# A fused attention and feed-forward kernel: its opening and first block reordered

## The chip, the cores and the metric

The kernel runs on 1 core of one Trainium2 chip. The metric is the device time of one execution, in microseconds (us). In the text PE is the matmul engine (TensorE), DVE, ACT and POOL are the vector, scalar and GpSimd engines, and SP is the engine that issues most data transfers (DMAs). POOL issues the weight transfers, which convert fp32 to bf16 on the way.

## The reference, cut to what matters

```python
# q, k, v: (B=8, H=8, S=576, D=64) fp32
def phi(x, c, s):                       # c, s: cos and sin of (pi/2) * pos / S
    r = np.maximum(x, 0.0)
    return np.concatenate([r * c, r * s], axis=-1)          # 64 -> 128 features
q_p = phi(q, cos_w, sin_w);  k_p = phi(k, cos_w, sin_w)
kv  = np.einsum('bhsf,bhsd->bhfd', k_p, v);  z = np.sum(k_p, axis=2)
num = np.einsum('bhsf,bhfd->bhsd', q_p, kv)
den = np.einsum('bhsf,bhf->bhs', q_p, z)[..., None] + 1e-06
x   = (num / den).transpose(0, 2, 1, 3).reshape(B * S, H * D)   # 4608 x 512
xn  = x / sqrt(mean(x * x) + 1e-06) * rms_g
out = (silu(xn @ w_gate) * (xn @ w_val)) @ w_out                # 512 -> 1536 -> 512
```

Each batch has 576 tokens: four chunks of 128 (c = 0 to 3) and a tail of 64 (c = 4).

## The kernel before

The feed-forward part (FFN) works in nine blocks of 512 tokens: one per batch, and a last one of the eight 64-token tails. A block has twelve gate/value steps (n = 0 to 11, eight matmuls of 128x512 each) and then 48 output matmuls. Attention for batch b+1 is computed inside block b, by small jobs that are hung into the steps. Block 0 has no block ahead of it, so an "opening" computes the attention of batch 0 first. Before block 1 can start, block 0 must also have produced the attention of batch 1.

The words used below: `phi` builds q or k features (on DVE and ACT); `kvz` is the key/value product; `nd` is the attention product of one q chunk, followed by `nd_post` (divide), `x_sq` (sum of squares on ACT, power on POOL), `x_norm` (DVE) and `x_tr` (transpose to feed the FFN). The q features must be transposed before `nd`; the result is the tile `qpT`. There are two ways to do it:

```python
def q_tr_dma(b, c):                    # a DMA does it, issued by SP; no engine computes
    nc.sync.dma_start_transpose(out=q_dst(b, c), in_=...)
def q_tr_pe(b, c, bank):               # PE does it, eight 128x128 matmuls into PSUM
    for h in range(H):
        nc.tensor.transpose(dst[:, h, 0:n], t[lo:hi, h, :], ident[lo:hi, lo:hi])
def q_tr_evac(eng, b, c, bank):        # and DVE or ACT copies the result out
    copy(eng, q_dst(b, c), dst[:, :, 0:n])
```

The opening, and the transfers that follow it:

```python
for which in ("k", "q", "v"):          # load batch 0, in this order, on SP
    ...
# ... [cut: k phi, q phi, all q chunks transposed with q_tr_pe]
v_cast(nc.gpsimd, 0, LOW)              # waits for v; the weight issues stand behind it on POOL
gval_slice(0, 256)                     # 12 weight transfers in all, 256 columns each
# ... [cut: kvz, then per 128 tokens: nd, norm, x_tr, open_ffn(j) = steps 0 and 1]

def first_loads_of_1():
    first = load_main("k", k, 1, bufs=two)
    tc.add_manual_dep(first.ins, weight_dmas[9].ins.name, SYNC_DEP, reason="after the weights")
    load_tail("k", k, 1); load("q", 1); load("v", 1)
    ...                                # then w_out in four transfers on POOL, after v
```

The output phase of block 0, in which batch 1's attention is finished:

```python
for n in range(NNT):
    # ... [cut]
    if n == 3:
        kvz_pe(1, psA); ...
    if n in (4, 6, 8, 10):
        nd_pe(1, j, psA); nd_post(1, j, psA); x_sq(1, j); x_norm(1, j)
    if n in (5, 7, 9, 11):             # one output step later, PE needs the result of that chain
        x_tr_pe(1, j, psV[j % 2][:, :]); x_tr_evac(A, 1, j, psV[j % 2][:, :])
    for j in ...: out_mm(0, j, n, banks0[j])
```

From block 1 on, q chunks are transposed by DMA. In the steady blocks the v casts ran on ACT at slot 15, `kvz` at step 6, and the `nd` jobs at steps 7, 9, 11 and 12.

Of the kernel before, what the change touches and what calls it, by code (L numbers as in the profile page):

```python
# [22 lines left out]
def kernel(  # L23
# [11 lines left out]
    nc = tc.nc  # L35
# [42 lines left out]
    def load_tail(which, src, b):  # L78
        lo = 64 * (b % 2)
        t = one.tile([P, H, D], FP32, name=f"r{which}t{b % 2}", tag=f"r{which}t{b % 2}")  # L80
        raw[(which + "t", b)] = t
        return nc.sync.dma_start(
            out=t[lo : lo + 64, :, :],
            in_=src[b, :, 512:576, :].rearrange("h s d -> s h d"),
        )
# [8 lines left out]
    for which in ("k", "q", "v"):  # L94
        bufs = two if which == "k" else one
        load_main(which, src_of[which], 0, (0, 4), bufs)
        load_main(which, src_of[which], 0, (4, 8), bufs)
        load_tail(which, src_of[which], 0)

    gb = one.tile([P, DM], FP32, name="gb")  # L100
    with nc.allow_non_contiguous_dma(reason="rms_g to all partitions"):
        nc.sync.dma_start(
            out=gb[:, :],
            in_=moe_rms_g.rearrange("(o d) -> o d", o=1).to_broadcast([P, DM]),
        )

# [44 lines left out]
    kpt = [one.tile([P, H, F], BF16, name=f"kpt{i}") for i in range(2)]  # L151
# [5 lines left out]
    for i in range(2):  # L157
        other = slice(64, 128) if i == 0 else slice(0, 64)
        mine = slice(0, 64) if i == 0 else slice(64, 128)
        nc.gpsimd.memset(kpt[i][other, :, :], 0.0)  # L160
        nc.gpsimd.memset(vvt[i][other, :, :], 0.0)
        nc.gpsimd.memset(vvt[i][mine, :, D:E], 1.0)
        nc.gpsimd.memset(vvm[i][:, :, :, D:E], 1.0)
# [15 lines left out]

    def half(b):  # L180
        lo = 64 * (b % 2)
        return lo, lo + 64
# [12 lines left out]
    def k_phi(eng, b, c, part, heads=(0, 8)):  # L195

        o = slice(0, D) if part == 0 else slice(D, F)
        f = cos_of if part == 0 else sin_of
        if c < 4:
            if b not in kp_main:  # L200
                kp_main[b] = one.tile([P, 4, H, F], BF16, name="kpm", tag="kpm")
            src = view4(raw[("k", b)], heads)[:, :, c, :]
            phi(eng, kp_main[b][:, c, heads[0] : heads[1], o], src, f(c))
        else:
            lo, hi = half(b)
            phi(eng, kpt[b % 2][lo:hi, :, o], raw[("kt", b)][lo:hi, :, :], f(4, lo, hi))

    def q_phi(eng, b, c, part, heads=(0, 8)):
        o = slice(0, D) if part == 0 else slice(D, F)
        f = cos_of if part == 0 else sin_of  # L210
        if (b, c) not in qp_tiles:
            qp_tiles[(b, c)] = four.tile([P, H, F], BF16, name="qp", tag="qp")
        t = qp_tiles[(b, c)]
        if c < 4:
            src = view4(raw[("q", b)], heads)[:, :, c, :]
            phi(eng, t[:, heads[0] : heads[1], o], src, f(c))
        else:
            lo, hi = half(b)
            phi(eng, t[lo:hi, :, o], raw[("qt", b)][lo:hi, :, :], f(4, lo, hi))

    def q_dst(b, c):
        if b not in qpT:
            qpT[b] = two.tile([P, H, S], BF16, name="qpT", tag="qpT")
        n = P if c < 4 else 64
        return qpT[b][:, :, c * P : c * P + n]

    def q_tr_dma(b, c):
        t = qp_tiles[(b, c)]
        lo, hi = (0, P) if c < 4 else half(b)
        nc.sync.dma_start_transpose(  # L230
            out=q_dst(b, c), in_=t[lo:hi, :, :].rearrange("p h f -> p (h f)")
        )

    def q_tr_pe(b, c, bank):
        t = qp_tiles[(b, c)]
        lo, hi = (0, P) if c < 4 else half(b)
        n = hi - lo
        dst = bank.bitcast(BF16).rearrange("p (h s) -> p h s", h=H)
        for h in range(H):
            nc.tensor.transpose(dst[:, h, 0:n], t[lo:hi, h, :], ident[lo:hi, lo:hi])  # L240

    def q_tr_evac(eng, b, c, bank):
        n = P if c < 4 else 64
        dst = bank.bitcast(BF16).rearrange("p (h s) -> p h s", h=H)
        copy(eng, q_dst(b, c), dst[:, :, 0:n])
# [14 lines left out]
    def v_cast_tail(eng, b):  # L260
        lo, hi = half(b)
        copy(eng, vvt[b % 2][lo:hi, :, 0:D], raw[("vt", b)][lo:hi, :, :])
# [4 lines left out]
    def kvz_pe(b, pst, heads=range(8)):  # L267
        o = headview(pst)
        for h in heads:
            for c in range(5):  # L270
                lhsT = kp_main[b][:, c, h, :] if c < 4 else kpt[b % 2][:, h, :]
# [10 lines left out]
    def nd_pe(b, j, pst):  # L282

        o = headview(pst)
        for h in range(H):
            g, i = h // 4, h % 4
            if j < 4:
                nc.tensor.matmul(  # L288
                    o[:, g, i, :], lhsT=qpT[b][:, h, j * P : (j + 1) * P],
                    rhs=kvzs[b][:, g, i * E : (i + 1) * E], start=True, stop=True,  # L290
                )
            else:
                for bb in (b - 1, b):
                    lo, hi = half(bb)
                    nc.tensor.matmul(
                        o[lo:hi, g, i, :], lhsT=qpT[bb][:, h, 512:576],
# [117 lines left out]
    def filler(n):  # L414
        for _ in range(n):
            nc.tensor.matmul(
                psO[:, 1, :], lhsT=warm[:, 0:P], rhs=warm[:, :], start=True, stop=True
            )


    V, A = nc.vector, nc.scalar
    LOW, HIGH = (0, 4), (4, 8)
    filler(24)
# [6 lines left out]
    qbank = [psG[0][:, :], psG[1][:, :], psV[0][:, :], psV[1][:, :], psO[:, 0, :]]  # L430
    for c in range(4):
        q_phi(V, 0, c, 0, LOW)
        q_phi(A, 0, c, 1, LOW)
    for c in range(4):
        q_phi(V, 0, c, 0, HIGH)
        q_phi(A if c < 2 else V, 0, c, 1, HIGH)
        q_tr_pe(0, c, qbank[c])
        if c >= 1:
            q_tr_evac(V, 0, c - 1, qbank[c - 1])
    v_cast(nc.gpsimd, 0, LOW)  # L440
# [7 lines left out]
    v_cast(V, 0, HIGH)  # L448
    v_cast_tail(A, 0)
    q_tr_evac(V, 0, 3, qbank[3])  # L450
    for i in range(1, 6):
        gval_slice(256 * i, 256 * i + 256)
    kvz_pe(0, psA, range(0, 4))
    kvz_evac(A, 0, psA, 0)
    kvz_pe(0, psA, range(4, 8))
    kvz_evac(A, 0, psA, 1)

    def open_tr(j):
        x_tr_pe(0, j, (psA if j % 2 == 0 else psO)[:, 0, :])
        x_tr_evac(A, 0, j, (psA if j % 2 == 0 else psO)[:, 0, :])  # L460

    def open_ffn(j):
        for n in range(2):
            gval_mm(0, n, n, (j * P, (j + 1) * P))

    nd_pe(0, 0, psA)
    filler(2)
    nd_post(0, 0, psA)
    x_sq(0, 0)
    nd_pe(0, 1, psO)  # L470
    nd_post(0, 1, psO)
    x_sq(0, 1)
    x_norm(0, 0)
    open_tr(0)
    nd_pe(0, 2, psA)
    open_ffn(0)
    nd_post(0, 2, psA)
    x_sq(0, 2)
    x_norm(0, 1)
    open_tr(1)  # L480
    nd_pe(0, 3, psO)
    open_ffn(1)
# [3 lines left out]
    open_tr(2)  # L486
    open_ffn(2)
    x_norm(0, 3)
    open_tr(3)
    open_ffn(3)  # L490
    q_phi(V, 0, 4, 0)
    q_phi(V, 0, 4, 1)
    q_tr_pe(0, 4, qbank[4])
    q_tr_evac(A, 0, 4, qbank[4])
    for n in range(2):
        gval_h(0, n, n, gval_act(0, n, n))
# [22 lines left out]
    def first_loads_of_1():  # L519
        first = load_main("k", k, 1, bufs=two)  # L520
        tc.add_manual_dep(first.ins, weight_dmas[9].ins.name, SYNC_DEP, reason="after the weights")
        load_tail("k", k, 1)
        load("q", 1)
        load("v", 1)
        for i in range(4):
# [5 lines left out]
            if i == 0:  # L531
                tc.add_manual_dep(
                    d.ins, last_load[("v", 1)].ins.name, SYNC_DEP, reason="after batch 1"
                )
# [6 lines left out]
    for c in range(5):  # L541
        at(0, 8 + (c + 1) // 2, "post", q_phi, V, 1, c, 0)
        at(0, 8 + (c + 1) // 2, "post", q_phi, A, 1, c, 1)
        n = (9, 10, 11, 12, 13)[c]
        at(0, n, "pe", q_tr_pe, 1, c, psA[:, c % 2, :])
        at(0, n, "pre", q_tr_evac, V, 1, c, psA[:, c % 2, :])
    at(0, 11, "post", v_cast, A, 1)
    at(0, 11, "post", v_cast_tail, A, 1)


    for nb in range(2, B):
        b = nb - 1
        first = nb == 2
        for c in range(5):
            kb, kn = (b, 1 + (c * 3) // 5) if first else (b - 1, 12 + (c * 3) // 5)
            at(kb, kn, "post", k_phi, V, nb, c, 0)
            at(kb, kn, "post", k_phi, A, nb, c, 1)
            qn = c + 3 if first else c
# [3 lines left out]
        vb, vn = (b, 5) if first else (b - 1, 15)  # L562
        at(vb, vn, "post", v_cast, A, nb, LOW)
        at(vb, vn + 1 if first else vn, "post", v_cast, A, nb, HIGH)
        at(vb, vn, "post", v_cast_tail, A, nb)
        kz = 8 if first else 6
# [3 lines left out]
        for j in range(4):  # L570
            n = ((9, 10, 11, 12) if first else (7, 9, 11, 12))[j]
# [11 lines left out]
    for nb in range(3, B):  # L583
# [3 lines left out]
        at(b, 7 if b == 1 else 2, "pre", load, "v", nb)  # L587
        at(b, 8 if b == 1 else 5, "post", load, "q", nb)

    def gval_step(blk, n):  # L590
        bank = n % 2
# [18 lines left out]
    for n in range(2, NNT):  # L610
        gval_step(0, n)
    banks0 = [psC[0][:, :], psC[1][:, :], psG[0][:, :], psG[1][:, :]]
    for n in range(NNT):
        if n == 0:
            run(0, 12, "pe")
            run(0, 12, "pre")
# [3 lines left out]
        if n == 2:  # L620
            run(0, 13, "pe")
            run(0, 13, "pre")
        if n == 3:
            kvz_pe(1, psA)
            kvz_evac(A, 1, psA, 0)
            kvz_evac(A, 1, psA, 1)
        if n in (4, 6, 8, 10):
            j = n // 2 - 2
            nd_pe(1, j, psA)
            nd_post(1, j, psA)  # L630
            x_sq(1, j)
            x_norm(1, j)
        if n == 5:
            load("v", 2)
            load("q", 2)
        if n in (5, 7, 9, 11):
            j = (n - 1) // 2 - 2
# [6 lines left out]
    run(0, 12, "post")  # L644
    run(0, 13, "post")
    run(0, 14, "post")
    run(0, 15, "post")
# [41 lines left out]
```

## Time and profile before

| | before |
|---|---|
| timed, median of 3 | 373.08 us (373.04 to 374.59) |
| the profiled execution | 369.74 us, of which the profile shows a span of 368.0 us |
| block 1 starts (first gate matmul of it) | 92.53 us |
| blocks 1 to 6 | 34.1, 35.2, 34.3, 35.2, 34.4, 35.2 us |
| blocks 7 and 8 (no attention in them) | 31.1 us each |

Block starts are read from PE's timeline: the first gate matmul after a run of output matmuls. First the head of the page: busy times, then PE's busy share and granted clock in 40 equal slices (9.2 us each), in tenths.

```profile
span 368.0 us, 5659 instructions
...
PE 330.5 (90%) x2122; PEld 163.8 (45%) x2122; DVE 179.4 (49%) x366; ACT 185.8 (50%) x345; POOL 37.7 (10%) x74
...
PE   7628797865999999999999999999999999999995
...
PEclk9655599988999999999999999999999999999999
```

PE is busy nearly everywhere but in the first ten slices. 90% alone would suggest that nothing is to be had; the slices show one poor stretch of 92 us and a dense remainder. What PE waited for in that stretch (engine, line, tile and releaser: us in total, times, longest):

```profile
PE psV L362 <- DVE xn L337: 8.8, 4, 2.7
PE psA L362 <- DVE xn L337: 5.8, 2, 5.6
PE psA L240 <- DVE qp L191: 2.7, 2, 1.3
```

The first line is the output phase of block 0, and the timeline shows one of its four links (start, duration, engine, line, what; in brackets the idle time before it):

```profile
71.21 0.42 PE L288 MATMUL psA<-kvzs,qpT 128*128 128x65 bf16 x8
...
71.73 0.17 DVE L309 TENSOR_SCALAR rec<-psA 128x8 f32<-128x8 f32 x1 [2.99 <-PE psA L288]
...
72.17 0.69 DVE L313 TENSOR_TENSOR xt<-psA,rec 128x512 f32<-128x512 f32 x1
72.96 0.64 ACT L325 ACTIVATE scr<-xt 128x513 bf16<-128x513 f32 x1 [1.80 <-DVE xt L313]
...
73.77 0.56 POOL L330 TENSOR_TENSOR rs<-ms,mhalf 128x1 f32<-128x1 f32 x1 [22.28 <-ACT scr L325]
74.36 0.75 DVE L337 SCALAR_TENSOR_TENSOR xn<-xt,rs,gb 128x512 bf16<-128x512 f32 x1 [1.50 <-POOL rs L330]
...
75.17 0.40 PE L362 MATMUL psV<-ident,xn 128*128 128x128 bf16 x4 [2.68 <-DVE xn L337]
```

From the attention product at 71.21 to the transpose that needs its result at 75.17 are 4.0 us, and PE has only one output step (four matmuls) to fill them with. It stands 2.7 us here, and 8.8 us in the four links together. The phase lasts from 66.06 to 92.53 us for 10.4 us of output matmuls; the waits cost clock as well (0.66 granted from 75 to 80 us).

The clock in that stretch, by windows (the columns are: window, length, busy time of PE, PEld, DVE, ACT, POOL with counts, granted PE clock, DMA share, GB/s):

```profile
10.00:15.00 5.00, 3.25 (x32) 2.61 (x33) 4.51 (x11) 1.13 (x4) 2.59 (x3) 0.63 1.00 266
...
25.00:30.00 5.00, 2.91 (x28) 2.48 (x28) 2.44 (x5) 1.10 (x2) 0.93 (x2) 0.50 1.45 196
...
45.00:50.00 5.00, 5.00 (x23) 2.19 (x22) 2.08 (x3) 1.42 (x3) 1.60 (x3) 0.96 0.14 28
```

The clock is halved from about 11 us (0.63 is the mean over 10 to 15 us) to about 45 us. The Trainium skill, "TensorE: Matmul & The Clock Gate", Part 1, says that the throttled clock is the default and that some 3.4 us of sustained activity release it. This trace agrees: matmuls run without a gap from 41.74 us, and the full clock is back at about 45.4 us.

In the steady blocks, PE's waits from 126.7 to 301 us are two groups, and the q transposes by DMA land in 4.0 us (median from issue to landing):

```profile
PE psA L288 <- DVE xt L313: 3.0, 5, 0.6
PE psG L376 <- ACT sg L385: 1.5, 3, 0.5
```
```profile
qpT<-qp SPq DMA_TRANSPOSE x25, 4.0
```

### The profile page before, as it was taken

To read this page: it belongs to the slowest core of one execution; us is meant where nothing else is said; L and a number is where in the kernel's file an instruction comes from. 1 tells how busy PE (TensorE), PEld (TensorE's weight loads), DVE (VectorE), ACT (ScalarE), POOL (GpSimd) and SP (SyncE) were. 2 spreads that over 40 slices of the span, in tenths; PEclk is the share of its full clock that TensorE was granted. 3 is DMA by queue.
4 is the path that set the end of the run, shared out by engine and by line. 5 is a ranking of instruction groups with operands and counts; after the bars stand their busy time and mean duration, and the time that the engine had idled before them with its cause. 6 is when DMAs were issued, how large, how long until landed. Compare 5 with 4: busy or idle time off the path is not lost.

```text
span 368.0 us, 5659 instructions
## 1 busy us (share of the span) xinstructions
PE 330.5 (90%) x2122; PEld 163.8 (45%) x2122; DVE 179.4 (49%) x366; ACT 185.8 (50%) x345; POOL 37.7 (10%) x74
## 2 busy tenths in 40 slices
PE   7628797865999999999999999999999999999995
PEld 3517443422454445445444544454445444444442
DVE  6635255433859266825772576358255723303320
ACT  5322265422884784576567556853694433313321
POOL 4651030011002000100110011001000110000000
PEclk9655599988999999999999999999999999999999
DMA  8999968630899799559956993999442250011013
GB/s 245 211 189 230 266 93 195 185 89 0 241 138 248 177 219 238 137 149 203 265 110 184 229 206 97 207 210 195 118 106 54 30 157 3 0 57 59 0 28 86
DMA packets 94875, 53.84 MB, mean 146 GB/s; under 512 B 57856, under 2 KB 90112, under 8 KB 94848
## 3 DMA queue, kind: packets, MB, share of 16 engines
q1 hardware_dynamic: 86912, 48.77, 57.3%
q0 software_dynamic: 7936, 4.72, 9.3%
q8 instruction: 16, 0.26, 0.3%
q14 instruction: 11, 0.09, 0.1%
HBM read 38.01 MB, written 9.44 MB: 129 GB/s over the span
## 4 chain that ended last, share of the span: by engine, by line
PE 69%; DVE 10%; ACT 8%; DMA 6%; issue 4%; POOL 2%; SPq 1%; ACTq 0%; DVEq 0%
PE psC L396 24%; PE psG L376 19%; PE psV L376 19%; DVE xn L337 3%; DVE xt L313 3%; PE psA L273 2%; DMA wv<-in_moe_w_val_dram 2%; DMA rv<-in_v_dram 2%; ACT vvm L249 2%; ACT scr L325 2%; PE psA L288 2%; ACT sg L385 1%; DMA rq<-in_q_dram 1%; PE psG L396 1%; DVE rec L312 1%
## 5 line engine op out<-in xcount | busy, mean ns | idle before, releaser
L391 DVE TENSOR_TENSOR hT<-psV,sg 128x512 bf16<-128x512 f32 x108 | 74.5, 690 | 121.4 <-PE psV L376 72.3
L376 PE MATMUL psG<-xnT,wg 128*128 128x512 bf16 (+1 forms) x408 | 102.4, 376 | 4.3 <-ACT sg L385 2.7
L376 PE MATMUL psV<-xnT,wv 128*128 128x512 bf16 (+1 forms) x408 | 102.5, 377 | 0.0
L385 ACT ACTIVATE sg<-psG 128x512 f32<-128x512 f32 x108 | 64.0, 594 | 64.9 <-PE psG L376 64.6
L396 PE MATMUL psC<-wo,hT 128*128 128x512 bf16 x408 | 92.8, 382 | 0.0
L376 PEld LDWEIGHTS <-wv 128*128 128x128 bf16 x456 | 45.4, 102 | 50.7 <-issue 1.1
L376 PEld LDWEIGHTS <-wg 128*128 128x128 bf16 x456 | 43.4, 101 | 49.5 <-issue 7.3
L396 PEld LDWEIGHTS <-hT 128*128 128x128 bf16 x432 | 41.4, 99 | 47.0 <-issue 1.1
L330 POOL TENSOR_TENSOR rs<-ms,mhalf 128x1 f32<-128x1 f32 x36 | 19.9, 555 | 236.4 <-ACT scr L325 236.4
L249 ACT COPY osb<-psC 128x512 f32<-128x512 f32 x33 | 19.3, 586 | 47.5 <-PE psC L396 47.5
L337 DVE SCALAR_TENSOR_TENSOR xn<-xt,rs,gb 128x512 bf16<-128x512 f32 x36 | 26.9, 746 | 21.8 <-POOL rs L330 21.8
L325 ACT ACTIVATE scr<-xt 128x513 bf16<-128x513 f32 x36 | 22.9, 636 | 24.7 <-DVE xt L313 24.5
L313 DVE TENSOR_TENSOR xt<-psA,rec 128x512 f32<-128x512 f32 x34 | 23.5, 691 | 1.2
L189 ACT ACTIVATE qp<-rq,tab 128x512 bf16<-128x512 f32 (+1 forms) x34 | 22.4, 676 | 0.8 <-DMA rq<-in_q_dram 0.7
L189 ACT ACTIVATE kpm<-rk,tab 128x512 bf16<-128x512 f32 (+1 forms) x34 | 21.0, 673 | 1.9 <-DMA rk<-in_k_dram 1.9
L288 PEld LDWEIGHTS <-qpT 128*128 128x128 bf16 x256 | 13.7, 104 | 14.4 <-issue 8.9
L288 PE MATMUL psA<-kvzs,qpT 128*128 128x65 bf16 x240 | 13.5, 201 | 4.7 <-DVE xt L313 3.6
L191 DVE TENSOR_SCALAR qp<-rq,tab 128x512 bf16<-128x512 f32 (+1 forms) x38 | 16.7, 454 | 0.7 <-DMA rq<-in_q_dram 0.7
L191 DVE TENSOR_SCALAR kpm<-rk,tab 128x512 bf16<-128x512 f32 (+1 forms) x38 | 15.2, 448 | 2.4 <-DMA rk<-in_k_dram 2.4
L249 ACT CAST vvm<-rv 128x1024 bf16<-128x1024 f32 (+1 forms) x13 | 14.0, 1113 | 0.1
L309 DVE TENSOR_SCALAR rec<-psA 128x8 f32<-128x8 f32 x34 | 5.5, 161 | 16.6 <-PE psA L288 14.5
L273 PEld LDWEIGHTS <-kpm 128*128 128x128 bf16 x256 | 11.6, 102 | 3.2 <-issue 1.5
(66 smaller groups left out, 177.3 us busy)
## 6 DMA issues: line engine op xcount, KB each, us to landing
out_dram<-osb SPq DMA_DIRECT2D x32, 256.0 KB, 2.4
rk<-in_k_dram SPq DMA_DIRECT2D x7, 1024.0 KB, 6.8
rq<-in_q_dram SPq DMA_DIRECT2D x7, 1024.0 KB, 7.1
rv<-in_v_dram SPq DMA_DIRECT2D x7, 1024.0 KB, 6.7
wg<-in_moe_w_gate_dram POOLq DMA_DIRECT2D x6, 256.0 KB, 8.9
wv<-in_moe_w_val_dram POOLq DMA_DIRECT2D x6, 256.0 KB, 9.6
wo<-in_moe_w_out_dram POOLq DMA_DIRECT2D x4, 384.0 KB, 6.9
rk<-in_k_dram SPq DMA_DIRECT2D x2, 512.0 KB, 4.4
```

Of the source, the lines that this page charges most:

```text
L189: nc.scalar.activation(out=out_ap, in_=in_ap, func=AF.Relu, scale=scale)
L191: nc.vector.tensor_scalar(out=out_ap, in0=in_ap, scalar1=scale, scalar2=0.0, op0=ALU.mult, op1=ALU.max)
L249: nc.scalar.copy(out=o, in_=i)
L288: nc.tensor.matmul(o[:, g, i, :], lhsT=qpT[b][:, h, j * P : (j + 1) * P], rhs=kvzs[b][:, g, i * E : (i + 1) * E], start=True, stop=True,)
L313: nc.vector.tensor_tensor(out=xt[:, 0:DM].rearrange("p (b h d) -> p b h d", b=2, d=D), in0=o[:, :, :, 0:D], in1=rec[:, :, :].unsqueeze(3). ...
L325: nc.scalar.activation(out=scr[:, :], in_=xt[:, 0 : DM + 1], func=AF.Square, scale=1.0 / math.sqrt(DM), accum_out=ms[:, :],)
L330: nc.gpsimd.tensor_tensor(out=rs[:, :], in0=ms[:, :], in1=mhalf[:, :], op=ALU.pow)
L337: nc.vector.scalar_tensor_tensor(out=xn[:, :], in0=x_of[(b, j)][:, 0:DM], scalar=rs_of[(b, j)][:, :], in1=gb[:, :], op0=ALU.mult, op1=ALU. ...
L376: nc.tensor.matmul(pst[bank][:, cols[0] : cols[1]], lhsT=w[:, t, n * P : (n + 1) * P], rhs=x[:, t, cols[0] : cols[1]], start=(t == 0), sto ...
L385: nc.scalar.activation(out=sg[:, :], in_=psG[bank][:, :], func=AF.Silu)
L391: nc.vector.tensor_tensor(out=hTs[blk][:, n, :], in0=psV[bank][:, :], in1=sg[:, :], op=ALU.mult)
L396: nc.tensor.matmul(bank, lhsT=hTs[blk][:, n, j * P : (j + 1) * P], rhs=wo[:, n, :], start=(n == 0), stop=(n == NNT - 1),)
```

## The change

The intent is to start the FFN sooner and to fill the gaps in block 0. It has six parts:

1. Batch 0 is loaded as k, v, q, with q by token pairs. Weights are issued when v has landed; there are 8 transfers (four of 256 columns, then four of 512) for 12.
2. The opening does FFN steps 0 to 3 (before: 0 and 1), with matmuls over 128 or 256 tokens, and ten dummy matmuls (fillers) in two groups stand between its attention products (before: two).
3. q chunks 2 and 3 of batch 0, its tail, and all q chunks of batch 1 are transposed by DMA, no longer by PE.
4. In block 0's output phase, `nd` comes at n = 1, 3, 5, 7 and each `x_tr` four or five output steps later.
5. The 64-token tails are laid out by head halves on 128 partitions.
6. In the steady blocks the v casts go from ACT to DVE and POOL, `kvz` to step 4, `nd` to steps 5, 7, 9, 11.

The diff, cut to its core (the tail layout and the new opening FFN helpers are left out):

```diff
-    for which in ("k", "q", "v"):
+    for which in ("k", "v"):
...
+    load_pair("q", 0, 0)
+    load_pair("q", 0, 1)
...
     gval_slice(0, 256)
+    tc.add_manual_dep(
+        weight_dmas[0].ins, first["v"].ins.name, SYNC_DEP, reason="weights after v"
+    )
+    gval_slice(256, 512)
...
+    for c in (2, 3):
+        q_phi(G, 0, c, 0)
+        q_phi(A, 0, c, 1)
+        q_tr_dma(0, c)
...
-    q_tr_pe(0, 4, qbank[4])
-    q_tr_evac(A, 0, 4, qbank[4])
+    q_tr_dma(0, 4)                       # on SP, ahead of batch 1's loads
...
     def first_loads_of_1():
-        first = load_main("k", k, 1, bufs=two)
-        tc.add_manual_dep(first.ins, weight_dmas[9].ins.name, SYNC_DEP, reason="after the weights")
+        d = load_main("k", k, 1, bufs=two)
+        tc.add_manual_dep(d.ins, weight_dmas[6].ins.name, SYNC_DEP, reason="after the weights")
         load_tail("k", k, 1)
         load("q", 1)
-        load("v", 1)
+        gate = load_main("v", v, 1, LOW)  # w_out is issued when this half has landed
+        load_main("v", v, 1, HIGH)
...
-        n = (9, 10, 11, 12, 13)[c]
-        at(0, n, "pe", q_tr_pe, 1, c, psA[:, c % 2, :])
-        at(0, n, "pre", q_tr_evac, V, 1, c, psA[:, c % 2, :])
+        n = (8, 8, 9, 9, 10)[c]
+        at(0, n, "post", q_tr_dma, 1, c)
...
-        at(vb, vn, "post", v_cast, A, nb, LOW)
-        at(vb, vn + 1 if first else vn, "post", v_cast, A, nb, HIGH)
+        at(vb, vn, "post", v_cast, V, nb, LOW)
+        at(vb, vn + 1, "post", v_cast, V, nb, HIGH)
...
-        if n in (4, 6, 8, 10):
-            j = n // 2 - 2
+        if n in (1, 3, 5, 7):
+            j = n // 2
             nd_pe(1, j, psA)
             nd_post(1, j, psA)
             x_sq(1, j)
-            x_norm(1, j)
...
-        if n in (5, 7, 9, 11):
-            j = (n - 1) // 2 - 2
+        if n in (4, 6, 8, 10):
+            x_norm(1, n // 2 - 2)
+        if n in (6, 8, 10, 11):
+            j = (6, 8, 10, 11).index(n)
             x_tr_pe(1, j, psV[j % 2][:, :])
```

## The prediction

> What bounds it now. The page says PE is busy 90% of 368.0 us. The table of windows and the chain of waits split that in two. In steady blocks PE is the bound: twelve gate/value steps of 1.73 us (8 matmuls) and 10.37 us of output matmuls are 31.1 us, and blocks 7 and 8, which carry no attention, take that. Blocks 2 to 6 take 34.4 or 35.2 us between the ends of their output matmuls, against about 33.7 of matmul work: 0.5 us at each block start waiting for the Silu behind two 1.04 us v casts and a 0.62 us tail cast on ACT, and about 0.6 to 0.9 us at the n=12 attention product waiting for DVE. The opening is the larger loss: block 1 starts at 92.5 us, though block 0 holds some 32 us of matmuls. There: v lands at 12.4 to 14.9 us and only then do weights start; first FFN matmul at 27.9; clock granted 0.50 from 13 to 45 us; q transposes starve PE at 55.8 to 65 (ACT and DVE phi work); the output phase of block 0 takes 66 to 92.5 us for 10.4 us of matmuls, because each link of norm, transpose and attention (about 5 us) is waited for in series.
>
> What the change does. v is loaded second and q last, so weights start at about 10 us instead of 13.4. The q load now overlaps them. Key/value product at about 11, first FFN at about 21 to 22 (estimate: the same DVE, ACT, POOL links, q landing at 12 to 15, two DMA transposes landing about 4 to 6 us after issue). The opening does steps 0 to 3 rather than 0 and 1, in wider 256-column matmuls. Step 4, at 47.2 before, should begin at about 36.
>
> What it costs. On the SP queue the loads of batch 1 now stand behind the tail-q DMA transpose, which waits for the last opening FFN product. So k of batch 1 is issued at about 38 (31.9 before), lands at about 44, q at about 48, v at about 52 (rates as before, 13 us for the three). Its phi work blocks the Silu queue: I expect PE to stall 2 to 5 us around step 8 and again near v. wo, gated on half of v, lands piecewise from about 55 to 60 (48.4 to 59 before).
>
> Output phase of block 0: attention products at n=1,3,5,7, transposes 5 steps later: about 14 us instead of 26. Block 1 then starts at about 69 (64 to 74), 23 us earlier.
>
> Steady: v cast goes to DVE (0.68 a half) and POOL, the attention products all lie in gate/value steps. Both measured stalls should go: about 1.1 us in each of 5 to 6 blocks, 6 us in all.
>
> The Trainium skill ("TensorE: Matmul & The Clock Gate", Part 1) says that the clock is halved by default and released after about 3.4 us of sustained activity. The trace agrees: continuous matmuls from 41.7, full clock by 45.3. A denser opening should regain it near 30.
>
> Sum: 373 - 23 - 6 = 344 us; 80% range 336 to 353. Faster by over 2%: 0.97; within 2%: 0.025; slower: 0.005.
>
> To check: weight issue near 10; step 4 near 36; k of batch 1 issued near 38 with ACT and DVE waiting for it; block 1 start near 69; blocks 2 to 6 near 33.8.
>
> Wrong if: DMA transposes stall the opening under weight traffic; the batch 1 loads come later than I think; PE stays at half clock through the stalls; or DVE becomes the releaser in steady blocks.

## The result, and the profile after

The changed kernel is correct and took 355.43 us (median of 4, 354.07 to 357.78), against 373.83 us for the kernel before in the same rounds. The ratio is 0.9508, with a 95% interval of 0.9443 to 0.9574. A ratio here is the mean time of one kernel's fast runs over that of the other's of the same rounds, so it is not quite the ratio of the medians. The direction was right; the time lies 11.4 us above the 344 predicted and 2.4 us above the range.

| us | before | predicted | after |
|---|---|---|---|
| first weight issue | 13.39 | about 10 | 11.14 |
| first gate/value matmul | 27.95 | 21 to 22 | 23.36 |
| step 4 starts | 46.98 (the prediction read 47.2) | about 36 | 38.11 |
| k of batch 1 issued | 31.89 | about 38 | 41.03 |
| output phase of block 0 | 26.5 | about 14 | 21.0 |
| block 1 starts | 92.53 | 69 | 80.87 |
| blocks 1 to 6 together | 208.5 | 6 less | 205.4 |
| span of the profile | 368.0 | | 353.1 |

The spans differ by 14.9 us, and the table accounts for that: 92.53 - 80.87 = 11.7 us ahead of block 1, and 208.5 - 205.4 = 3.2 us (from the unrounded block times) in the steady blocks. The timed medians differ by more, 18.4 us, because the profiled execution of before was one of its faster ones (369.74 us against a median of 373.83). Block 1 starts 11.9 us after the 69 us predicted, and of the 6 us after it 2.8 us are missing. In sum that is more than the 11.4 us by which the timed median missed, for the same reason: the trace of before is of one of its faster executions.

The head of the page after:

```profile
span 353.1 us, 5619 instructions
...
PE 321.0 (91%) x2052; PEld 159.3 (45%) x2087; DVE 180.0 (51%) x369; ACT 165.4 (47%) x323; POOL 39.0 (11%) x85
...
PE   8557958399899999999899999999999999999994
...
PEclk9976989789999999999999999999999999999999
```

The half-clock stretch of the opening has shrunk from some 34 us to about ten (22 to 32 us), but PE still has holes: the 5s in slices 2, 3 and 6, and the 3 in slice 8. What it waited for ahead of block 1:

```profile
PE psA L302 <- DMA qpT<-qp: 9.7, 3, 5.4
PE psG L391 <- ACT sg L400: 3.9, 1, 3.9
...
PE psO L302 <- DMA qpT<-qp: 1.4, 1, 1.4
```

The waits for DVE's `xn` are gone but for 0.2 us, as intended. In their place are 11.1 us of waits for `qpT` that come from a DMA, which the kernel before did not have ahead of block 1: 3.5 and 1.4 us in the opening, 0.8 and 5.4 us in the output phase. The 3.9 us line is the predicted stall in which ACT, holding batch 1's k features ahead of a Silu, waits for k.

Now the transfers. The issues on SP (start, how long SP was held, what), then those on POOL:

```profile
15.28 5.24 SPq L243 DMA_TRANSPOSE qpT<-qp  x2
39.74 1.19 SPq L243 DMA_TRANSPOSE qtT<-qp  x1
41.03 0.54 SPq L73 DMA_DIRECT2D rk<-in_k_dram  x1
...
53.87 14.88 SPq L243 DMA_TRANSPOSE qpT<-qp  x4
```
```profile
11.14 0.95 POOL L185 DMA_DIRECT2D wg<-in_moe_w_gate_dram  x1 [7.14 <-DMA rvt<-in_v_dram]
...
53.76 3.09 POOL L579 DMA_DIRECT2D wo<-in_moe_w_out_dram  x4 [23.05 <-DMA rv<-in_v_dram]
```

Two things stand in those lines. The tail transpose (`qtT`) is issued at 39.74 and k of batch 1 right behind it, so the end of the opening decides when batch 1 begins to load. And the four q transposes of batch 1 are issued at 53.87, a tenth of a microsecond after the four w_out transfers at 53.76; the issues alone take 14.88 us. The landing times (issue to landing, median) in two windows, 9 to 53 us and 46 to 76 us:

```profile
wg<-in_moe_w_gate_dram POOLq DMA_DIRECT2D x2, 512.0 KB, 10.8
wv<-in_moe_w_val_dram POOLq DMA_DIRECT2D x2, 512.0 KB, 10.6
...
qpT<-qp SPq DMA_TRANSPOSE x2, 9.1
qtT<-qp SPq DMA_TRANSPOSE x1, 3.4
```
```profile
wo<-in_moe_w_out_dram POOLq DMA_DIRECT2D x4, 384.0 KB, 9.6
...
qpT<-qp SPq DMA_TRANSPOSE x4, 9.9
```

A q transpose takes 9.1 or 9.9 us where weights are under way, 3.4 us where nothing much is (the tail, with half of the data), and took 4.0 us in the steady blocks of before. The w_out transfers took 6.9 us before and 9.6 now. How full the DMA engines are does not tell the two cases apart: their busy share (the sum of the packets' times, which can pass 1) is 1.10 from 53.9 to 70.8 us, and it was 1.13 to 1.16 in before while the q transposes of blocks 2 to 5 landed beside loads of k, q and v. Those loads are issued by SP, as the transposes are; the weights are issued by POOL. The long wait also costs clock:

```profile
65.00:70.00 5.00, 0.84 (x9) 0.57 (x10) 0.17 (x1) 0.00 (x0) 0.00 (x0) 0.61 1.17 200
70.00:75.00 5.00, 4.95 (x27) 2.29 (x27) 3.08 (x7) 1.07 (x3) 0.55 (x1) 0.71 0.89 235
```

Between 65 and 70 us PE is nearly idle and the DMA engines are fully busy. In the steady part, the waits from 80.9 to 185.3 us are

```profile
PE psA L302 <- DMA qpT<-qp: 1.9, 2, 1.1
PE psA L287 <- DVE vvm L261: 1.0, 1, 1.0
```

and from 185.3 to 286 us there are none. Blocks 4 to 6 take 33.8, 33.3 and 33.8 us, 3.9 us less than before in sum; blocks 1 to 3 (34.9, 34.8, 34.7) gained nothing (0.7 us more in sum).

### The profile page after: what moved, and what is told of

Its sections match the earlier page's. It is cut to its first block, busy times and chain, and to the rows that moved or that the text cites. A ratio compares the mean times of both kernels' runs of the same rounds, so it can differ in the third digit from the quotient of the medians.

```text
span 353.1 us, 5619 instructions
## 1 busy us (share of the span) xinstructions
PE 321.0 (91%) x2052; PEld 159.3 (45%) x2087; DVE 180.0 (51%) x369; ACT 165.4 (47%) x323; POOL 39.0 (11%) x85
## 4 chain that ended last, share of the span: by engine, by line
PE 76%; DMA 15%; DVE 2%; ACT 2%; SPq 2%; issue 2%; ACTq 0%; DVEq 0%
PE psC L411 25%; PE psG L391 22%; PE psV L391 21%; DMA qpT<-qp 11%; PE psA L302 2%; DMA rq<-in_q_dram 2%; PE psA L287 2%; DMA rkt<-in_k_dram 2%; PE psG L411 1%; PE psG L496 1%; SPq L82 1%; SPq L73 1%; PE psV L496 1%; DVE qp L203 1%; PE psO L496 1%
## 5 line engine op out<-in xcount | busy, mean ns | idle before, releaser
L406 DVE TENSOR_TENSOR hT<-psV,sg 128x512 bf16<-128x512 f32 x104 | 71.7, 690 | 103.9 <-PE psV L391 78.7
L391 PE MATMUL psG<-xnT,wg 128*128 128x512 bf16 x351 | 93.1, 382 | 4.6 <-ACT sg L400 3.9
L391 PE MATMUL psV<-xnT,wv 128*128 128x512 bf16 x365 | 94.6, 382 | 0.4
L400 ACT ACTIVATE sg<-psG 128x512 f32<-128x512 f32 x104 | 61.8, 594 | 69.3 <-PE psG L391 68.1
L391 PEld LDWEIGHTS <-wv 128*128 128x128 bf16 x416 | 40.9, 98 | 49.7 <-issue 1.1
L391 PEld LDWEIGHTS <-wg 128*128 128x128 bf16 x416 | 38.8, 98 | 46.6 <-issue 5.3
L302 PE MATMUL psA<-kvzs,qpT 128*128 128x65 bf16 x240 | 13.1, 197 | 11.5 <-DMA qpT<-qp 11.5
L201 ACT ACTIVATE qp<-rq,tab 128x512 bf16<-128x512 f32 x32 | 22.4, 713 | 1.2 <-DMA rq<-in_q_dram 1.2
L302 PEld LDWEIGHTS <-qpT 128*128 128x128 bf16 x256 | 12.2, 101 | 23.3 <-DMA qpT<-qp 16.5
L203 DVE TENSOR_SCALAR qp<-rq,tab 128x512 bf16<-128x512 f32 x32 | 15.4, 490 | 2.1 <-DMA rq<-in_q_dram 2.1
L287 PEld LDWEIGHTS <-kpm 128*128 128x128 bf16 x256 | 10.6, 97 | 6.0 <-issue 4.5
L287 PE MATMUL psA<-vvm,kpm 128*128 128x65 bf16 x256 | 11.1, 193 | 2.0 <-DVE vvm L261 1.8
```

Source lines behind the costliest of these rows:

```text
L201: nc.scalar.activation(out=out_ap, in_=in_ap, func=AF.Relu, scale=scale)
L203: nc.vector.tensor_scalar(out=out_ap, in0=in_ap, scalar1=scale, scalar2=0.0, op0=ALU.mult, op1=ALU.max)
L287: nc.tensor.matmul(o[:, h // 4, h % 4, :], lhsT=lhsT, rhs=rhs, start=(c == 0), stop=(c == 4))
L302: nc.tensor.matmul(o[:, g, i, :], lhsT=qpT[(b, 0)][:, h, j * P : (j + 1) * P], rhs=kvzs[b][:, g, i * E : (i + 1) * E], start=True, stop=True,)
L391: nc.tensor.matmul(pst[bank][:, cols[0] : cols[1]], lhsT=w[:, t, n * P : (n + 1) * P], rhs=x[:, t, cols[0] : cols[1]], start=(t == 0), sto ...
L400: nc.scalar.activation(out=sg[:, :], in_=psG[bank][:, :], func=AF.Silu)
```

## The experiments

The theory, called T in the texts: q transposes by DMA that run beside bulk transfers slow down and slow those transfers (what the runs show, below, is narrower: beside weights), in the opening and again beside w_out; and the tail transpose ahead of k's load ties batch 1 to the end of the opening. The rivals (R, and later R2) put the loss, or what remained of it, elsewhere; each text says what its rival expects.

A run over 1.5% above the fastest of its kernel is called slow and left out of the ratios, but not of the medians. Medians below are of four runs, unless said otherwise, and each call ran on one chip beside the kernel before, whose medians were 370.3, 372.17 and 370.11 us. The same kernel on two chips agreed to 0.3% (355.43 and 356.51 us for the changed one, 342.30 and 342.07 for a variant below), while single runs of the kernel before ranged from 366.9 to 375.6 us; so medians of variants are compared directly, and the ratios to before are given with their intervals. These are wide: the ratio of the changed kernel itself moved from 0.9508 to 0.9619 (after_again below), so for a difference of 1% between variants the traces weigh more than the times.

### e1_loads_first: batch 1's loads ahead of the tail transpose

```diff
     q_phi(V, 0, 4, 1)
-    q_tr_dma(0, 4)
...
     first_loads_of_1()
+    q_tr_dma(0, 4)
```

> The loads of batch 1 are issued before the DMA transpose of batch 0's q tail. Theory T (what cost the missing 11 us is mainly that q is transposed by DMA while weights are moving): k of batch 1 is issued near 30 us instead of 41.0, the 3.9 us Silu wait and the half clock after it go (-5 to -6 us), but the four q transposes of batch 1 still overlap wo, still land 8 us or more after issue, and PE still waits for qpT by 2 us or more; about 349 us. Rival R (the late loads of batch 1 are the whole miss; transposes are slow only because everything is late): wo is over before the transposes are issued, no wait for qpT above 1 us, about 344 us.

Measured: 349.98 us, ratio 0.9436 (0.9386 to 0.9486). This fits T's 349; if the order on SP were the whole loss, 344 would have come. The text expected k of batch 1 near 30 us, which did not come. The profiled execution fell in the slow state (354.05 us; the median of the other three is 349.19), so only its order is used: k of batch 1 was issued at 36.92 us instead of 41.03, now held by its other gate, a weight transfer, and the stall on k is no longer among PE's waits, while the waits for `qpT` are. So the order on SP is one part of the loss, worth some 5 to 7 us by the medians (the interval of the ratio still overlaps a little with the first of the changed kernel's two), and not all.

### e2_batch1_on_pe: batch 1's four main q chunks transposed by PE again

```diff
-        at(0, n, "post", q_tr_dma, 1, c)
+        if c < 4:
+            m = (10, 10, 11, 11)[c]
+            at(0, m, "pe", q_tr_pe, 1, c, psA[:, c % 2, :])
+            at(0, m, "pre", q_tr_evac, V, 1, c, psA[:, c % 2, :])
+        else:
+            at(0, n, "post", q_tr_dma, 1, c)
```

> The four full q transposes of batch 1 go back to PE (in gate/value steps 10 and 11), the loads stay late. T: the 0.8 and 5.4 us waits for qpT and the half clock from 69 to 73 go, k's wait at 45 to 49 stays; block 1 starts 6 to 8 us earlier, about 348 us. R: PE then waits for wo or for the late v instead; at most 2 us gained, 353 us or more.

Measured: 355.38 us, ratio 0.9587 (0.9540 to 0.9634). Where the edit acts, it did its work: block 1 starts at 75.66 us, 5.2 earlier, and w_out lands in 7.4 us where it took 9.6. But the total did not move, a clear miss for T; the rival's number (353 or more) came, though not by its waits. Block 1 grew from 34.9 to 38.6 us and block 2 from 34.8 to 36.1: PE waits there for the q transposes of batch 2 (from 75 to 115 us):

```profile
PE psA L302 <- DMA qpT<-qp: 3.5, 2, 2.1
```

The loads of batch 2 wait for w_out. k of batch 2 was issued 2.2 us earlier than in the changed kernel (67.99 against 70.16), block 1 started 5.2 us earlier, so it came nearer to its data, and the gain was given back one block later.

### e3_batch0_on_pe: q chunks 2 and 3 of batch 0 transposed by PE

```diff
     for c in (2, 3):
         q_phi(G, 0, c, 0)
         q_phi(A, 0, c, 1)
-        q_tr_dma(0, c)
     ...
     nd_pe(0, 0, psA)
+    q_tr_pe(0, 2, psV[0][:, :])
+    q_tr_pe(0, 3, psG[1][:, :])
     filler(4, idle)
     nd_post(0, 0, psA)
     x_sq(0, 0)
+    q_tr_evac(A, 0, 2, psV[0][:, :])
+    q_tr_evac(A, 0, 3, psG[1][:, :])
```

(Two x transposes also swap their PSUM banks, so that they do not meet these.)

> The q transposes of batch 0, chunks 2 and 3, go back to PE with their copies on ACT. T: the 3.5 and 1.4 us waits for qpT at 19 to 27 us go, step 4 starts 3 to 4 us earlier (34 to 35 us instead of 38.1) and all behind it moves too, since the loads of batch 1 hang on the end of the opening; about 352 us. R: the opening is limited by the chain of norm and attention or by weights landing; under 1 us gained, 354 to 355 us.

Measured: 351.78 us, ratio 0.9503 (0.9454 to 0.9552), as T expected (352). By the medians that is 4 to 5 us less than the changed kernel; the ratio alone does not set it apart from that kernel's first (0.9443 to 0.9574). The trace does: the first gate/value matmul comes at 21.32 us (21 to 22 predicted), step 4 starts at 31.64 us instead of 38.11, and block 1 at 73.41, 7.5 us earlier. T had expected only 3 to 4 us at step 4. Its total came out all the same because blocks 1 to 6 gave 3.5 us back (208.9 us against 205.4): the agreement at 352 is in part luck. The landing times in the opening, with the transposes of chunks 2 and 3 gone:

```profile
wg<-in_moe_w_gate_dram POOLq DMA_DIRECT2D x2, 512.0 KB, 6.7
wv<-in_moe_w_val_dram POOLq DMA_DIRECT2D x2, 512.0 KB, 8.7
```

They were 10.8 and 10.6 us in the changed kernel. This shows the second half of the coupling: two DMA transposes held up the weights too. Four traces have exactly the same opening code with the transposes in it (the changed kernel, its repeat, e2 and e6 below). In them the transposes took 9.1, 9.6, 10.0 and 11.2 us in the median, and the two late `wg` transfers 10.8, 11.5, 12.5 and 13.9: the more of the one, the more of the other. Why the amount differs from run to run stays open.

### e4_three: the three edits together

The edit is the sum of the three above.

> All three edits. T: the gains add, less 1 to 2 us of overlap: about 340 us, block 1 starting at 65 to 67 us, no PE wait for qpT before block 1. R: no better than e1 by more than 2 us.

Measured: 342.30 us, ratio 0.9239 (0.9183 to 0.9296). Repeated later on another chip as e4_again:

> The three edits again, so that the next two have it on the same chip. Ratio to before 0.92 to 0.935, block 1 about 39 us.

Measured: 342.07 us, ratio 0.9266 (0.9222 to 0.9311). Its trace comes close to what the prediction had said of the change itself, or runs ahead of it: block 1 starts at 63.2 us (69 predicted), the output phase takes 13.0 us, and the clock is full throughout the opening, here in the window where the changed kernel has 0.67:

```profile
20.00:25.00 5.00, 3.15 (x50) 2.91 (x50) 3.51 (x9) 3.06 (x8) 2.62 (x4) 1.00 1.23 185
```

The three edits together took 13 us off, while alone they took about 5, 0 and 4 (from the first median of the changed kernel). As the traces read, they act in series on one path: the opening frees the loads of batch 1 (k issued at 29.29 us instead of 41.03), these free w_out and the output phase, and that frees batch 2 (its k issued at 55.58 instead of 70.16). No run takes the links one by one. What remains is block 1, which now takes 39.3 us, with this wait:

```profile
PE psA L302 <- DMA qpT<-qp: 2.9, 1, 2.9
```

### after_again: the changed kernel again

No edit.

> The changed kernel as it is, on the chip and beside the runs of before that the next three share. Every theory: ratio to before 0.951 within its old interval.

Measured: 356.51 us, ratio 0.9619 (0.9547 to 0.9691); block 1 starts at 80.93 us (80.87 in the first trace). The ratio did not stay in its old interval (0.9443 to 0.9574), as the text expected, though the two intervals overlap; the kernel before ran faster (372.17 us against 373.83), the changed one 0.3% slower.

### e5_batch2_too: e4, and batch 2's q chunks by PE one step after their features

```diff
-            at(b, qn, "post", q_tr_dma, nb, c)
+            if late and c < 4:
+                at(b, qn + 1, "pe", q_tr_pe, nb, c, psC[c % 2][:, :])
+                at(b, qn + 1, "pre", q_tr_evac, V if c % 2 == 0 else A, nb, c, psC[c % 2][:, :])
+            else:
+                at(b, qn, "post", q_tr_dma, nb, c)
```

> The three edits together, and batch 2's four full q transposes on PE as well (through the two output banks, which are free then; copies shared by DVE and ACT). Theory T (DMA transposes beside bulk loads are the cost): block 1, 39.4 us long with the three edits, falls to 35 to 36 us and the whole to about 337 us. Rival R2 (block 1 is long because q of batch 2 lands late, whatever transposes it): block 1 stays above 38 us, 340 us or more.

Measured: 344.94 us, ratio 0.9319 (0.9231 to 0.9407). A miss: block 1 got longer, 41.1 us. The wait shows why:

```profile
PE psC L251 <- DVE qp L203: 5.4, 4, 1.3
```

A PE transpose one step after the features were queued comes before DVE has made them, so PE stood up to 1.3 us, four times. The wait for the DMA was exchanged for a wait of my own making; this run does not speak for or against the theories.

### e9_batch2_two_steps: e4, and the same two steps after

The edit is that of e5 with `qn + 2` for `qn + 1`.

> The three edits with batch 2's four full q transposes on PE, this time two gate/value steps behind their phi work instead of one, so that PE does not wait 1.3 us four times for DVE as in the first try. Theory T: block 1 falls from 39 to 35 to 36.5 us, 3 us less than the three edits alone. Rival R2 (q of batch 2 itself is too late): block 1 stays above 38 us.

Measured: 338.53 us (median of 6, 337.67 to 340.57), ratio 0.9175 (0.9131 to 0.9218). Block 1 takes 36.1 us instead of 39.3, and no wait for `qpT` is among PE's waits up to its end. So making batch 2's transposes by DMA did lengthen block 1, by 3.2 us. Slow landing is not shown to be the reason: in e4_again these four landed in 4.8 us (median, 3.2 to 7.4), against the 4.0 of the steady blocks. The first of them also stood in SP's queue. Its features were done at 71.46 us, but SP was held by the transpose of the 64-token tails' `xn`, and PE got the result at 79.19:

```profile
71.90 2.20 SPq L371 DMA_TRANSPOSE xnt_tail<-xn  x1
74.27 2.72 SPq L243 DMA_TRANSPOSE qpT<-qp  x1
```

Of those 7.7 us, 2.8 passed before the issue. This kernel is correct and faster than the kernel before and the changed one: the best.

### e6_wo_after_transposes: the changed kernel, w_out held until batch 1's q transposes have landed

```diff
     for n in range(4, NNT):
         gval_step(0, n, (n + 1) % 2)
+    load_wo(tr_of[(1, 3)])     # the w_out transfers, gated on the fourth q transpose
```

> The changed kernel (q transposes still by DMA), with the four wo transfers held back until batch 1's last full q transpose has landed, so that those transposes run without weight traffic. Contention theory: each of the four lands about 4 to 5 us after its issue (9.9 us median, 13.8 at most, in the changed kernel), the four issues take 7 us or less instead of 14.9, and the wait for qpT in the output phase is under 1 us; PE waits for wo instead, so the time is within 3 us of the changed kernel's. Rival (DMA transposes of this size queued four deep are slow by themselves): still 8 us or more to landing.

Measured: 360.12 us, ratio 0.9768 (0.9716 to 0.9820). It was not meant to be faster; the point is what lands when (first the SP timeline, then landing times from 46 to 76 us):

```profile
56.72 5.52 SPq L245 DMA_TRANSPOSE qpT<-qp  x4
```
```profile
wo<-in_moe_w_out_dram POOLq DMA_DIRECT2D x4, 384.0 KB, 7.0
...
qpT<-qp SPq DMA_TRANSPOSE x4, 3.4
```

The same four transposes, of the same data in the same block, land in 3.4 us instead of 9.9 (9.7 to 10.2 in the traces of after_again, e1 and e3, where they too run beside w_out), and their issues hold SP for 5.52 us instead of 14.88. They were not alone: loads issued by SP were still under way beside the first three, and the DMA engines' busy share from 56.7 to 64.3 us was 1.12. So it is the weights beside them that count, and not that the engines are full. Whether that is so because the weights go out on POOL's queue, because they are converted on the way, or for another reason, no run here tests. The w_out transfers land in 7.0 us instead of 9.6. Each slowed the other, and taking them apart restores both. No wait for `qpT` is left in the output phase, but PE then waits 6.2 us for w_out instead of the 5.4 us for `qpT`, so order alone wins nothing here. The total, expected within 3 us of the changed kernel's, came out 4.7 us above its first median and 3.6 above its second; it can't be compared closely: its opening, with the same code, issued the tail transpose at 43.45 us instead of 39.74, the variation told under e3.

### e7_old_steady: e4 with the old schedule of the steady blocks

(The diff is condensed.)

```diff
-        vb, vn = (b, 3) if late else (b - 1, 14)
+        vb, vn = (b, 3) if late else (b - 1, 15)
-        (v casts on V, V and G;  kz = 4, nds = (5, 7, 9, 11))
+        (v casts on A, A and A;  kz = 6, nds = (7, 9, 11, 12);  batch 2 unchanged)
```

> The three edits, with the old steady schedule for batches 3 to 7 (v cast on ACT in slot 15, tail cast on ACT, key/value product at step 6, attention products at 7, 9, 11 and the first output step). If the steady gain is what I read before (0.5 us at the block start and 0.6 to 0.9 us at the attention product in the output phase), blocks 2 to 6 grow from 33.8 to about 34.8 to 35.2 us: about 6 us more than the three edits alone, 347 to 349 us. Rival: blocks 2 to 6 of the changed kernel are shorter for another reason (smaller tails), and under 2 us come back.

Measured: 346.95 us, ratio 0.9346 (0.9274 to 0.9419), 4.7 us above e4. Blocks 2 to 6 take 175.0 us in its trace, against 170.5 and 169.3 in the two traces of e4. PE's waits after block 1 are those of the kernel before again:

```profile
PE psA L302 <- DVE xt L328: 3.0, 5, 0.6
PE psG L391 <- ACT sg L400: 2.5, 5, 0.7
```

So the steady part of the change is worth 4.5 to 5.7 us when its inputs come in time, near the 6 predicted. In the changed kernel it gave only 3.2, because the first blocks wait for late transposes.

### e8_old_output_phase: e4 with the old order in block 0's output phase

(The diff is condensed.)

```diff
-        if n in (1, 3, 5, 7):     (nd;  x_norm at 4, 6, 8, 10;  x_tr at 6, 8, 10, 11)
+        if n in (4, 6, 8, 10):    (nd and x_norm;  x_tr at 5, 7, 9, 11)
```

> The three edits, with the output phase of block 0 in its old order (attention products at n = 4, 6, 8, 10, each transpose one n later). If the new order is what shortened that phase, it grows from 12.6 us to 20 or more, most of it idle PE with waits for xn: 8 to 10 us more than the three edits alone, about 351 us. Rival (the phase was long before because wo landed late or the clock was low): under 3 us more.

Measured: 350.74 us, ratio 0.9461 (0.9391 to 0.9531). The old wait returns in full,

```profile
PE psV L377 <- DVE xn L352: 9.2, 4, 2.7
```

and the phase takes 27.1 us again (50.28 to 77.39), so the reorder is worth 14 us where it stands. But the total rose by only about 8.4 us, because block 1 shrank from 39.3 to 34.7: with more time, the data of batch 2 was there. The same give and take as in e2, seen from the other side.

### e10_no_fillers: e4 without the fillers of the opening (dummy matmuls that keep PE active)

```diff
     nd_pe(0, 0, psA)
-    filler(4, idle)
...
     nd_pe(0, 1, psO)
-    filler(6, idle)
```

> The three edits without the two groups of filler matmuls in the opening (4 and 6). If they hold the clock: the granted clock falls to 0.5 somewhere between 17 and 33 us, step 4 starts 2 to 4 us later and so does all behind it. Rival (the denser opening keeps the clock by itself): under 1 us of change.

Measured: 343.62 us, ratio 0.9289 (0.9235 to 0.9344), beside e4_again's 342.07 on the same chip; the intervals overlap, so the time is inconclusive. The clock is not:

```profile
20.00:25.00 5.00, 3.54 (x36) 3.42 (x36) 2.72 (x7) 2.49 (x6) 2.62 (x4) 0.50 1.22 191
```

It fell to 0.50 from 20 to 25 us, where e4_again has 1.00, and block 1 started 1.3 us later (64.51 against 63.19), less than the 2 to 4 expected. The fillers are worth 1.3 us of block 1's start in these two traces; a gain in the total is not shown.

## Why the prediction was right or wrong

**Right: the direction, and what would be removed.** The waits for DVE's `xn` went. Weights are issued at 11.14 us (about 10 said). The stall on k came, 3.9 us, within the 2 to 5 said. Blocks 4 to 6 run at 33.8, 33.3 and 33.8 us.

**Wrong: the cost of the DMA transposes.** The step that failed reads "two DMA transposes landing about 4 to 6 us after issue", together with the tacit one that the transposes of batch 1 cost nothing. The 4 us came from the steady blocks, where the median is 4.0 (2.8 to 8.8 us) beside loads of k, q and v, and was moved to two places where the traffic beside them is weights. There they took 9.1 us (opening) and 9.9 us (beside w_out), and held up those weights: 10.8 and 10.6 us (`wg`, `wv`) against 6.7 and 8.7 without them, and w_out 9.6 against 7.0. e3 shows the effect on the weights, e6 shows both at once. The Trainium skill, "DMA: Bandwidth & Descriptors", sections "Queues, rings and completion order" and "Issuing engines are not separate DMA queues", says that transfers of all issuing engines share the same 16 DMA engines and that each engine serves its queue rows in turn, packet by packet. The runs agree that a transpose from SP and a weight from POOL are not independent; they do not show the packets in turn. The prediction listed "DMA transposes stall the opening under weight traffic" under what would make it wrong, without a number in the sum.

**The size of it.** Of the 11.9 us missing at the start of block 1, step 4 is late by 2.1 us (38.11 against 36), the output phase is 7.0 us longer than the 14 said (waits of 0.8 and 5.4 us for `qpT`, then half clock to about 72 us), and the remaining 2.8 us lie between, in the steps 4 to 11 with the stall on k. The 2.1 us hide a larger error: with the opening's transposes on PE (e3) step 4 starts at 31.64 us, 4.4 us ahead of the prediction, so the prediction had estimated the rest of the opening too long, and the two errors partly cancelled. With the three edits of e4 that remove the transposes from the crowded places and their order ahead of k, block 1 starts at 63.2 us, ahead even of the 69 predicted.

**Half wrong: the loads of batch 1.** The prediction saw that k of batch 1 would stand behind the tail transpose, and said 38 us; it was 41.03, because the opening ended later. So the transposes of the opening cost twice: once in the opening, and once through that order. e1 puts the order at some 5 to 7 us.

**Half wrong: the steady gain.** 6 us were predicted, 3.2 came. e7 shows 4.5 to 5.7 for that part where its inputs come in time. In blocks 1 to 3 of the changed kernel PE waits for `qpT` (1.9 us) and for v's cast (1.0 us), which took the place of the old waits.

**Missed altogether: what is won early can be given back.** e2, e4 and e8 show that block 1 lengthens when it starts sooner, because its own inputs, loaded behind w_out, are then the limit. The prediction carried every microsecond of block 1's start straight to the end. In the changed kernel that nearly held (block 1 took 34.9 us, 34.1 before), but only because block 1 started late: when it started at 63.2 us it took 39.3.

**The range** of 336 to 353 was too narrow for a sum that rested on a landing time taken from a stage with other traffic.

## What to carry to other kernels

Cost a transfer from a trace of the stage in which it will run, with the kind of traffic that will be beside it: the same DMA transposes took 3.4 us with the weights held back and 9.9 us next to them, at much the same busy share of the DMA engines, and they slowed the weights as well. Where PE has gaps anyway, as in an opening, a transpose on PE may be the cheap one, provided it stands far enough behind the instruction that makes its input (two steps won here, one step lost). And before you add an early gain to the total, ask which data the next stage needs and when it lands.

## What the Trainium skill lacked or had wrong

- "DMA: Bandwidth & Descriptors" gives an effective rate for DMA transposes, but neither its section "DMA Transpose (X-bar)" nor "Latency and other measured facts" says what one takes under load. The runs show a median of 3.4 us (four chunk transposes with w_out held back) and 9.9 us (the same four beside w_out), with 5.52 and 14.88 us of SP's time for their issues.
- The same page, "Rules for kernel authors", says that "A transpose next to ordinary DMAs needs nothing". That stands among rules about correctness, and every variant here was correct, but for time it misleads: weights of 512 KB took 10.8 and 10.6 us (`wg`, `wv`) beside two transposes and 6.7 and 8.7 us without, w_out 9.6 and 7.0 us.
- The same page, under "Alternative transpose paths", says of TensorE only that it is "useful when data already on-chip"; that it also spares the weights beside it is not said. Here, moving ten chunk transposes of batches 0, 1 and 2 to PE, together with one change of order, took 355.43 us to 338.53.
